# Four block products of a first group's second matmul in seven products instead of eight, with their operand sums made by accumulating DMAs

## The chip, the cores and the metric

The kernel runs on one core of one Trainium2 chip. The metric is the device time of one launch in microseconds; the figure given for a kernel is the median of its runs.

## What is computed

Two stages, in fp32. Attention with routing: queries and keys are assigned to the nearest of 16 centroids, and a query attends only to keys of its own cluster. Then an MLP on the attention's output, and it is this part that the change touches:

```python
x = attn_out.transpose(0, 2, 1, 3).reshape(3072, 512)
h = x @ w_in                                   # w_in: 512 x 2048
g = np.where(h > 0, h, np.exp(np.minimum(h, 0)) - 1)
return g @ w_out                               # w_out: 2048 x 512
```

## The kernel before

After the attention, the 3072 tokens are worked off in six groups of 512, `k_` = 0 to 5. Each group has a first product (`x @ w_in`, with the ELU behind it) and a second product (`g @ w_out`, with a store of the result).

Both products use Strassen's scheme in Winograd's form: a product of two 2x2 block matrices in seven block products instead of eight. `w_out` is kept as seven "quads", which are the right operands of the outer level: `a11`, `a12`, `s1`, `a22` lie in place in the tile `w_out`, and `s2`, `s4`, `s3` lie in parts of the tiles `p_out`, `sums_w` and `words_w`. So a group's second product is seven *units* `UNITS` (n = 0 to 6: M1 with `a11`, M2 with `a12`, M3 with `s4`, M7 with `s3`, M6 with `s2`, M5 with `s1`, M4 with `a22`). A unit is again a 2x2 block product, of 512-deep blocks with 128 columns, and it can be done in two ways:

- *plainly*, in eight small products: for each of four quadrants `q_`, two small products accumulate in a PSUM bank. A small product (`small_product`, line 1042) is four matmuls of 128x128 by 128x128.
- *in sevenths*, by the same scheme once more (`OutUnit`, `chain`): the small products m1 to m7, with sums of the four parts q11, q12, q21, q22 of the left operand (`t_step`, t1 to t4, VectorE) and of the right operand: s1 = q21 + q22, s2 = s1 - q11, s3 = q11 - q21, s4 = q12 - s2. m1, m2 and m4 take q11, q12 and q22 themselves; m5, m6, m7 and m3 take s1, s2, s3 and s4. `chain` interleaves the units: m6, m2, the next unit's m1, m7, the next unit's m5, m3, m4.

In the kernel before, the second product of group 0 is plain throughout (`second_product_plain`), and those of groups 1 to 5 run in sevenths. The right-hand sums of the quads ("`w_out`'s table") are made once, by VectorE, during the first product of group 1 (`table_steps`: seven quads of four operations, two steps at each call of `fill`), and stored to HBM by SyncE's DMA queue (`keep_far`). From then on they are streamed back into ten slots. `s1` overwrites q21 in its quad. A second table, of `w_in`, serves the first products of groups 2 to 5. It is made during the second product of group 0 (`in_table_steps`, 16 VectorE operations, 13 stores and 4 loads on SyncE's queue), with the tile `spare` and the dead columns of `xT` for its results.

The order of the work is written by hand (a manual schedule): each engine runs its own instructions in program order and waits only for what they depend on. A DMA waits on the queue of the engine that issues it, so what stands behind it on that engine waits too. SyncE (SP) issues plain loads and stores, GpSimd (POOL) some others.

Around the change stand: `early_on`, which ends the preparation of `w_out`'s quads in unit 0; `verdict`, a 1x1 matmul in unit 2; `take`, which empties the quadrants' banks into `s_all` (ScalarE for M1, M3, M7) or adds to the output (VectorE); `g_step`, which updates the outer left operands in place; and `next_group(0)` after unit 5, which makes the left sums of group 1's first product in the tile `x_sum` (`x_sum_step`, four POOL operations) and loads its first right-hand sums into `w_tmp` (`w_step`, three SP loads; `w_tmp` is the first half of `spare`, `stage` the second). The first product of group 1 (`unit`) is four units of seven block products (line 796).

Of the kernel before, what the change touches and what calls it, by code (L numbers as in the profile page):

```python
# [14 lines left out]
Act = mybir.ActivationFunctionType  # L15
Alu = mybir.AluOpType
# [3 lines left out]
P = 128  # L20
# [41 lines left out]
def main_path(ctx, tc, c, q, k, v, centroids, moe_w_in, moe_w_out, out):  # L62


    nc = tc.nc
# [7 lines left out]
    KC = DM // P  # L73
    FC = DF // P
    N = B * S
    GS = 512
# [17 lines left out]
    xT = space.tile([P, KC, N], F32, name="xT")  # L94
# [811 lines left out]
    def part_w(a, i, j):  # L906
        return quad_w[a][:, 4 * j : 4 * j + 4, ts(i, P)]

    def part_g(b, i, j):
        return quad_g[b][:, 4 * i : 4 * i + 4, ts(j, P)]  # L910
# [12 lines left out]
    def flat_far(a, x):  # L923
        return far_w[a, x].rearrange("p (f m) -> p f m", m=P)

    def table_steps():


        made = []

        def keep_far():
            for to, src in made:
                nc.sync.dma_start(to, src)
            made.clear()

        for n, a in enumerate(("s3", "s4", "s2", "a11", "a12", "s1", "a22")):
            at = p_out[:, :1536] if n % 2 else s_all
            s3, s2, s4 = (at[:, ts(m, 512)].rearrange("p (f m) -> p f m", m=P) for m in range(3))
            q11, q12, q21, q22 = (part_w(a, i, j) for i in range(2) for j in range(2))
            nc.vector.tensor_tensor(s3, q11, q21, op=Alu.subtract)  # L940
            yield
            nc.vector.tensor_tensor(q21, q21, q22, op=Alu.add)
            keep_far()
            yield
            nc.vector.tensor_tensor(s2, q21, q11, op=Alu.subtract)
            yield
            nc.vector.tensor_tensor(s4, q12, s2, op=Alu.subtract)
            parts = [("s3", s3), ("s2", s2), ("s4", s4)]
            if a not in DIRECT:
                parts += [("q11", q11), ("q12", q12), ("q22", q22), ("s1", q21)]  # L950
            made += [(flat_far(a, x), y) for x, y in parts]
            yield
        keep_far()

    WHICH = {"m1": "q11", "m2": "q12", "m3": "s4", "m4": "q22", "m5": "s1", "m6": "s2", "m7": "s3"}
    HERE = {"m1": (0, 0), "m2": (0, 1), "m4": (1, 1), "m5": (1, 0)}
# [3 lines left out]
    FIRST_IN = 2  # L960
# [12 lines left out]

    def in_table_steps():

        dead = [xT[:, ch, :GS] for ch in range(KC)]
        flat = spare.rearrange("p a n -> p (a n)")
        held = [flat[:, ts(n, 512)] for n in range(6)]
        made = []

        def keep_far():
            for to, src in made:
                nc.sync.dma_start(to, src)
            made.clear()

        for a, s1, (s3, s2, s4) in (
            ("a11", dead[0], held[3:]),
            ("s1", dead[0], dead[1:]),
            ("a12", held[0], held[3:]),
            ("s2", dead[2], held[:3]),  # L990
        ):
            if a == "s2":
                keep_far()
                for n in range(4):
                    nc.sync.dma_start(dead[n], s2_far[:, n // 2, n % 2])
                q11, q12, q21, q22 = dead
            else:
                q11, q12, q21, q22 = (part_in(a, i, j) for i in range(2) for j in range(2))
            nc.vector.tensor_tensor(s3, q11, q21, op=Alu.subtract)
            yield  # L1000
            nc.vector.tensor_tensor(s1, q21, q22, op=Alu.add)
            keep_far()
            yield
            nc.vector.tensor_tensor(s2, s1, q11, op=Alu.subtract)
            yield
            nc.vector.tensor_tensor(s4, q12, s2, op=Alu.subtract)
            made += [(far_in[a, x], y) for x, y in (("s3", s3), ("s2", s2), ("s4", s4))]
            if a == "s2":
                made.append((far_in[a, "s1"], s1))
            yield  # L1010
        keep_far()
# [16 lines left out]
    def weights(of, a, m):  # L1028

        nonlocal used  # L1030
        table = far_w if of == "out" else far_in
        if (a, WHICH[m]) not in table:
            i, j = HERE[m]
            return (part_w if of == "out" else part_in)(a, i, j), lambda: None
        assert streamed[used] is table[a, WHICH[m]]
        slot_ = slots_w[used % len(slots_w)]
        used += 1
        return slot_.rearrange("p (f m) -> p f m", m=P) if of == "out" else slot_, fetch
# [12 lines left out]
    def banks_of(k_, n):  # L1051
        return sets[(k_ + n) % 2]
# [5 lines left out]
    class OutUnit:  # L1058
        of, width = "out", P

        def __init__(self, k_, n):
            self.k_, self.n, self.a = k_, n, UNITS[n][1]
            self.banks = [x[:, :P] for x in banks_of(k_, n)]
            self.m5 = stage[:, 2, ts(n % 2, P)]
            self.u3 = stage[:, 2, 256 + P * (n % 2) : 384 + P * (n % 2)]

        def product(self, m):
            left = t_of[SUM[m]] if m in SUM else part_g(UNITS[self.n][2], *SIDE[m])
            right, done = weights("out", self.a, m)
            small_product(self.banks[BANK[m]], left, right, m in ("m1", "m5"))  # L1070
            done()

        def t(self, t):
            t_step(self.n, t)

        def take(self, q_):
            take(self.k_, self.n, q_)

        def taken(self):
            taken(self.k_, self.n)  # L1080

        def note(self, at):
            k_, n = self.k_, self.n
            if at == "m2" and 1 <= n <= 3:
                g_step(n - 1, 0)
            elif at == "m7" and 1 <= n <= 3:
                g_step(n - 1, 1)
            elif at == "m4" and n == 1:
                next_group(k_)
            elif k_ + 1 == FIRST_IN and at in ("m2", "m7") and n in (4, 5):  # L1090
                x_sum_step(k_ + 1, 2 * (n - 4) + (at == "m7"))
            if at == "m4" and k_ == FIRST_IN - 1 and n < 3:
                in_place(n)
# [209 lines left out]

            behind.append(rest)

    def t_step(n, t):
        b = UNITS[n][2]
        q11, q12, q21, q22 = (part_g(b, i, j) for i in range(2) for j in range(2))
        to = t_of[t]
        if t == "t1":  # L1310
            nc.vector.tensor_tensor(to, q12, q11, op=Alu.subtract)
        elif t == "t2":
            nc.vector.tensor_tensor(to, q22, t_of["t1"], op=Alu.subtract)
        elif t == "t3":
            nc.vector.tensor_tensor(to, q22, q12, op=Alu.subtract)
        else:
            nc.vector.tensor_tensor(to, q21, t_of["t2"], op=Alu.subtract)
# [50 lines left out]
    def store(k_, tiles):  # L1368
        for i in range(2):
            store_tile(k_, 2 * tiles + i, nc.sync)  # L1370

    def next_group(k_):
        if k_ + 1 < N // GS:
            if k_ + 1 != FIRST_IN:
                for n in range(4):
                    x_sum_step(k_ + 1, n)
            for n in range(3):
                if n or k_ + 1 < FIRST_IN:
                    w_step(k_ + 1, 0, n)

    def second_product_plain(k_, early_on):

        in_table = in_table_steps()
        for n in range(len(UNITS)):
            _, a, b = UNITS[n]
            for q_ in range(4):
                for j in range(2):
                    small_product(
                        banks_of(k_, n)[q_],
                        part_g(b, j, q_ % 2),  # L1390
                        part_w(a, q_ // 2, j),
                        j == 0,
                        j == 1,
                    )
                if n == 0 and q_ == 0:
                    flush_all()
                    early_on()
                elif n == 2 and q_ == 1:
                    verdict()
                take(k_, n, q_)  # L1400
                if q_ < 3 and n > 0:
                    next(in_table, None)
            taken(k_, n)
            if n < 3:
                g_step(n, 0)
                g_step(n, 1)
            if n == 5:
                run(in_table)
                next_group(k_)

    def findings():
        ok = c["ok"]
# [55 lines left out]
    def run(steps_of):  # L1468
        for _ in steps_of:
            pass  # L1470
# [12 lines left out]
    for u in range(4):  # L1483
# [5 lines left out]
        elif u == 2:  # L1489
            scale_x(last_n - 1, r_of)  # L1490
            scale_x(last_n, e_of)
    second_product_plain(0, early_on)

    table = table_steps()

    def fill_table():
        next(table, None)
# [2 lines left out]
    for k_ in range(1, N // GS):  # L1500
        if k_ < FIRST_IN:
            for u in range(4):
                if u < 2:
                    blanks((k_ + u) % 2)
                run(unit(k_, u, fill=fill_table))
        else:
            rest_of_group(k_)
        chain(units_behind(k_))
# [261 lines left out]
```

## Time and profile before

| | us |
|---|---|
| median of 3 runs (lowest, highest) | 892.48 (892.21, 892.85) |
| profiled execution: its own time | 893.83 |
| profiled execution: its span, first to last instruction | 892.10 |

| share of the span | PE | VectorE | ScalarE | POOL |
|---|---|---|---|---|
| busy | 99% | 79% | 49% | 25% |

The second product of group 0 runs from 381.45 to 432.34 us of the span, and group 1's first product from there to 482.59 us. The profile is of one execution. A busy PE is read from the starts of its instructions, since their ends are modelled. A wait is charged to the engine or the DMA whose signal came last.

### The profile page before, as it was taken

Reading aid. Unit: us, or ns where it says so; the run is one execution under the profiler, and the core shown is the slowest. Engines: PE = TensorE matmul, PEld = TensorE weight load, DVE = VectorE, ACT = ScalarE, POOL = GpSimd, SP = SyncE. Lnnn points to the kernel's source line nnn. Section 1 sums busy time; section 2 is a strip of 40 time slices with the busy share of each in tenths; the row PEclk is TensorE's granted clock in tenths of the full one; section 3 lists DMA queues with packets and bytes.
Section 4 is the critical chain, followed back from the end, with each engine's and each line's share of the span. In section 5 each row is a group of like instructions: output and inputs, shape, how many; then the busy total and the mean of one; then the engine's idle time right before and its main releaser. Section 6 shows DMA issues by size and latency. Waiting matters only on the chain.

```text
span 892.1 us, 17029 instructions
## 1 busy us (share of the span) xinstructions
PE 880.4 (99%) x6473; PEld 681.1 (76%) x6473; DVE 705.5 (79%) x1021; ACT 440.4 (49%) x833; POOL 225.7 (25%) x289
## 2 busy tenths in 40 slices
PE   8999999999999999999999999999999999999997
PEld 5444444444444458899989999999999999999997
DVE  4789998999998987894588956894689568956784
ACT  5677786787768664410133236423642354225421
POOL 1011121121113566860123003510351025202300
PEclk9999999999999999999999999999999999999999
DMA  7766685466337442113597866186618661866172
GB/s 222 182 128 184 148 179 129 128 120 150 78 119 212 125 142 65 48 47 119 197 323 247 269 215 189 47 268 206 193 48 264 213 195 48 260 212 202 49 228 83
DMA packets 155257, 144.63 MB, mean 162 GB/s; under 512 B 89760, under 2 KB 107168, under 8 KB 154144
## 3 DMA queue, kind: packets, MB, share of 16 engines
q1 hardware_dynamic: 151584, 132.45, 50.1%
q0 software_dynamic: 3296, 10.49, 4.6%
q8 instruction: 53, 0.87, 0.4%
q10 hardware_dynamic: 288, 0.52, 0.2%
q14 instruction: 36, 0.29, 0.1%
HBM read 114.59 MB, written 21.50 MB: 153 GB/s over the span
## 4 chain that ended last, share of the span: by engine, by line
PE 91%; POOL 3%; DVE 2%; issue 2%; DMA 1%; SPq 1%; ACT 0%; POOLq 0%; ACTq 0%
PE bank L1042 23%; PE banks L510 15%; PE o_bank L548 14%; PE bank L796 11%; PE bank L1114 9%; PE o_bank L1042 4%; PE banks L523 4%; PE d_bank L1042 2%; PE o_bank L796 2%; PE o_bank L1114 2%; PE d_bank L568 1%; PE d_bank L438 1%; POOL kq_g L810 1%; PE d_bank L1114 1%; DMA spare<-w_far 1%
## 5 line engine op out<-in xcount | busy, mean ns | idle before, releaser
L532 ACT ACTIVATE p_out<-banks 128x768 f32<-128x768 f32 x192 | 154.0, 811 | 25.4 <-PE banks L523 23.7
L548 PE MATMUL o_bank<-p_out,kq_g 128*64 128x384 f32 x768 | 130.9, 490 | 0.0
L548 PEld LDWEIGHTS o_bank<-p_out,kq_g 128*64 128x64 f32 x768 | 52.3, 137 | 74.8 <-issue 69.7
L810 POOL TENSOR_SCALAR kq_g<-kq_g 128x512 f32<-128x512 f32 x96 | 69.4, 731 | 150.1 <-ACT kq_g L809 149.7
L535 DVE TENSOR_TENSOR sums_w<-p_out 128x1536 f32<-128x1536 f32 x32 | 59.1, 1847 | 10.3 <-ACT p_out L532 10.3
L1042 PE MATMUL bank<-w_out,kq_g 128*128 128x128 f32 x512 | 63.1, 275 | 0.3 <-DVE kq_g L813 0.3
L1042 PEld LDWEIGHTS bank<-w_out,kq_g 128*128 128x128 f32 x512 | 60.5, 192 | 0.8 <-DVE kq_g L813 0.5
L796 PE MATMUL bank<-xT,spare 128*128 128x256 f32 x256 | 59.3, 379 | 0.8 <-DMA spare<-w_far 0.8
L809 ACT ACTIVATE kq_g<-bank 128x512 f32<-128x512 f32 x68 | 39.8, 602 | 38.5 <-PE bank L796 18.4
L540 DVE TENSOR_TENSOR sums_w<-sums_w,p_out 128x1536 f32<-128x1536 f32 x32 | 56.2, 1757 | 3.3 <-DVE sums_w L535 0.5
L609 POOL DMA_DIRECT2D sums_w<-xT x28 | 17.8, 650 | 153.2 <-DVE xT L585 92.0
L796 PEld LDWEIGHTS bank<-xT,spare 128*128 128x128 f32 x256 | 48.2, 190 | 7.5 <-ACT kq_g L809 1.2
L796 PE MATMUL bank<-x_sum,w_in 128*128 128x256 f32 x224 | 52.9, 379 | 0.0
L813 DVE SCALAR_TENSOR_TENSOR kq_g<-kq_g,bank 128x512 f32<-128x512 f32 x68 | 45.0, 680 | 7.7 <-POOL kq_g L810 7.7
L796 PEld LDWEIGHTS bank<-x_sum,w_in 128*128 128x128 f32 x224 | 42.6, 190 | 5.8
L1328 DVE TENSOR_TENSOR kq_g<-kq_g 128x1024 f32<-128x1024 f32 x36 | 45.3, 1264 | 1.5 <-PE bank L1042 1.5
L1132 POOL TENSOR_TENSOR spare<-x_sum 128x128 f32<-128x128 f32 x16 | 7.3, 457 | 154.4 <-PE bank L1114 88.7
L562 ACT ACTIVATE xT<-o_bank 128x384 f32<-128x384 f32 x32 | 15.7, 489 | 53.0 <-PE o_bank L548 53.0
L604 POOL TENSOR_TENSOR xT<-xT,sums_w 128x384 f32<-128x384 f32 x32 | 41.1, 1305 | 1.6 <-DMA sums_w<-xT 1.6
L510 PE MATMUL banks<-x_sum,xT 64*128 64x384 f32 x192 | 39.8, 492 | 0.0
L510 PE MATMUL banks<-kq_g,xT 64*128 64x384 f32 x192 | 39.6, 491 | 0.0
L510 PE MATMUL banks<-x_sum,kq_g 64*128 64x384 f32 x192 | 39.6, 491 | 0.0
(343 smaller groups left out, 1998.8 us busy)
## 6 DMA issues: line engine op xcount, KB each, us to landing
kq_g<-in_v_dram SPq DMA_DIRECT2D x32, 384.0 KB, 3.7
sums_w<-far_s_s SPq DMA_DIRECT2D x42, 256.0 KB, 3.7
spare<-w_far SPq DMA_DIRECT2D x32, 256.0 KB, 3.2
words_w<-far_s_s SPq DMA_DIRECT2D x26, 256.0 KB, 3.1
out_dram<-p_out SPq DMA_DIRECT2D x22, 256.0 KB, 3.4
w_out<-in_q_dram SPq DMA_DIRECT2D x112, 48.0 KB, 2.4
sums_w<-xT POOLq DMA_DIRECT2D x28, 192.0 KB, 3.3
sums_w<-far_s_q SPq DMA_DIRECT2D x21, 256.0 KB, 3.5
```

The source lines that it names most:

```text
L510: nc.tensor.matmul(s[:, e, :HS], lhsT=kT[b % 2][pr][rows, ts(kt, P)], rhs=qT[half][pr][rows], start=True, stop=False,)
L532: nc.scalar.activation(probs[kt], s[:, :, :HS], Act.Exp, scale=SCALE)
L535: nc.vector.tensor_tensor(add_to, probs_all[:, : 4 * HS], probs_all[:, 4 * HS : 8 * HS], op=Alu.add)
L540: nc.vector.tensor_tensor(add_to, add_to, probs_all[:, 8 * HS :], op=Alu.add)
L548: nc.tensor.matmul(o_bank[64 * e : 64 * e + 64, :HS], lhsT=v_raw[n % 2][:, e, kt], rhs=probs[kt][:, e], start=(kt == 0), stop=(kt == NT - 1),)
L604: nc.gpsimd.tensor_tensor(x_of(n), x_of(n), r, op=Alu.mult)
L796: nc.tensor.matmul(bank[:, ts(f, QS)], lhsT=left[:, ch, ts(f, P)], rhs=right[:, ch], start=first and f == 0 and ch == 0, stop=ch == 1, ski ...
L810: nc.gpsimd.tensor_scalar(to, to, 1.0, 0.0, op0=Alu.min, op1=Alu.max)
L813: nc.vector.scalar_tensor_tensor(to, to, -1.0, as_part(bank, to), op0=Alu.add, op1=Alu.max)
L1042: nc.tensor.matmul(bank[:, :P], lhsT=left[:, f], rhs=right[:, f], start=first and f == 0, stop=last and f == 3, skip_group_check=True,)
L1114: nc.tensor.matmul(bank[:, ts(f, P)], lhsT=left[:, ts(f, P)], rhs=right, start=m in ("m1", "m5") and f == 0, stop=True, skip_group_check=True,
L1328: nc.vector.tensor_tensor(b[to][:, f], b[x][:, f], b[y][:, f], op=op)
```

## The change

Units 0 to 2 of group 0's second product stay plain (`second_product_first`). Units 3 to 6 run in sevenths, through `chain`. Their left sums t1 to t4 lie in dead columns of `xT` (`t_first`). Their right sums are made before they are needed:

- for `s3` (unit 3) by four VectorE operations in units 1 and 2 (`table_block`);
- for `s2` and `s1` (units 4, 5), and in part for `a22` (unit 6), by `tables_apart` after unit 0: seven negated copies on ScalarE and twelve accumulating DMAs on POOL's queue, each of 128x512 fp32 (256 KB);
- the rest of `a22` by `table_last`, at unit 4's m4: two negated copies and two accumulating DMAs.

The sums of these four quads go to HBM from here: 20 stores on SP's queue. The table of `w_in` moves into group 1's first product, behind the remaining three blocks of `w_out`'s table (`table_rest`), with its four loads and 13 stores; its results now lie in `p_out` and `s_all` instead of `spare`. `next_group(0)` stands at unit 5's m4.

```diff
+    made = []
+    def keep_far():
...
+    def table_block(a, at):
+        s3, s2, s4 = (x.rearrange("p (f m) -> p f m", m=P) for x in at)
+        q11, q12, q21, q22 = (part_w(a, i, j) for i in range(2) for j in range(2))
+        nc.vector.tensor_tensor(s3, q11, q21, op=Alu.subtract)
+        yield
+        nc.vector.tensor_tensor(q21, q21, q22, op=Alu.add)
+        keep_far()
+        yield
+        nc.vector.tensor_tensor(s2, q21, q11, op=Alu.subtract)
+        yield
+        nc.vector.tensor_tensor(s4, q12, s2, op=Alu.subtract)
...
+    late = [stage[:, 0], sums_w[:, 3584:], stage[:, 1]]
+    apart = {
+        "s2": [in_rows(x) for x in thirds(x_sum)],
+        "s1": [w_tmp[:, m].rearrange("p c n -> p (c n)") for m in range(3)],
+        "a22": [sums_w[:, 3584:], p_out[:, 4096:], stage[:, 0]],
+    }
...
+    def minus_of(to, x):
+        nc.scalar.activation(to, x, Act.Copy, scale=-1.0)
+    def add_far(to, x):
+        nc.gpsimd.dma_start(to, x, accum_op=Alu.add)
+    def tables_apart():
+        for a in ("s2", "s1"):
             q11, q12, q21, q22 = (part_w(a, i, j) for i in range(2) for j in range(2))
+            s3, s2, s4 = apart[a]
+            minus_of(s3, q21)
+            minus_of(s2, q11)
+            minus_of(s4, q22)
+            here[a].update(s2=s2, s3=s3, s4=s4)
+        q11, q12, q21, q22 = (part_w("a22", i, j) for i in range(2) for j in range(2))
+        minus_of(apart["a22"][1], q11)
+        for a in ("s2", "s1"):
...
+            add_far(q21, q22)
+            add_far(s3, q11)
+            add_far(s4, q12)
+        add_far(part_w("a22", 1, 0), part_w("a22", 1, 1))
+        for a in ("s2", "s1"):
+            s3, s2, s4 = apart[a]
+            add_far(s2, part_w(a, 1, 0))
+            add_far(s4, s3)
+        add_far(apart["a22"][1], part_w("a22", 1, 0))
+    def table_last():
+        s3, s2, s4 = apart["a22"]
+        minus_of(s3, s2)
+        minus_of(s4, s2)
+        add_far(s3, part_w("a22", 1, 1))
+        add_far(s4, part_w("a22", 0, 1))
...
+    def table_rest():
+        for n in range(4):
+            nc.sync.dma_start(dead[n], s2_far[:, n // 2, n % 2])
+        for a, at in (
+            ("s4", thirds(s_all)),
+            ("a11", thirds(p_out)),
+            ("a12", thirds(s_all)),
+        ):
+            yield from table_block(a, at)
+        yield from in_table_steps()
...
         def note(self, at):
+            if k_ == 0:
+                if at == "m4":
+                    if n == 3:
+                        g_step(2, 1)
+                        keep_far()
+                    elif n == 4:
+                        table_last()
+                        keep_apart("s2")
+                        keep_apart("s1")
+                    elif n == 5:
+                        keep_apart("a22")
+                        next_group(0)
+                return
...
+    FIRST_OUT = 3
+    first_table = table_block("s3", late)
+    def second_product_first(early_on):
+        for n in range(FIRST_OUT):
...
+                take(0, n, q_)
+                if n == 1 and q_ < 3 or n == 2 and q_ == 0:
+                    next(first_table, None)
+                if n == 2:
+                    t_step(FIRST_OUT, f"t{q_ + 1}", t_first)
+            taken(0, n)
+            if n == 0:
+                tables_apart()
+            for part in range(2 - n // 2):
+                g_step(n, part)
+        chain([(OutUnit, 0, n) for n in range(FIRST_OUT, len(UNITS))])
...
-    second_product_plain(0, early_on)
-
-    table = table_steps()
+    second_product_first(early_on)
+    table = table_rest()
```

More of the change, by code (lines that the diff above doesn't have):

```diff
@@ L924, in flat_far @@
         return far_w[a, x].rearrange("p (f m) -> p f m", m=P)
[L926 to L938, printed above, removed]
-            q11, q12, q21, q22 = (part_w(a, i, j) for i in range(2) for j in range(2))
[L940 to L952, printed above, removed]
-        keep_far()
+    made = []
@@ new lines, in keep_far @@
+    def keep_far():
+        for to, src in made:
+            nc.sync.dma_start(to, src)
+        made.clear()
+    def table_block(a, at):
[9 more added lines that the diff above has]
+        nc.vector.tensor_tensor(s4, q12, s2, op=Alu.subtract)
+        parts = [("s3", s3), ("s2", s2), ("s4", s4)]
+        here[a].update(parts)
+        if a not in DIRECT:
+            parts += [("q11", q11), ("q12", q12), ("q22", q22), ("s1", q21)]
+        made.extend((flat_far(a, x), y) for x, y in parts)
+        yield
@@ new lines, in main_path, with thirds, in_rows @@
+    here = {a: {} for a in quad_w}
+    dead = [xT[:, ch, :GS] for ch in range(KC)]
+    t_first = {
+        f"t{n + 1}": x.rearrange("p (f n) -> p f n", n=P) for n, x in enumerate(dead)
+    }
+    def thirds(x):
+        return [x[:, ts(m, 512)] for m in range(3)]
+    def in_rows(x):
+        return x.rearrange("p (f m) -> p f m", m=P)
+    late = [stage[:, 0], sums_w[:, 3584:], stage[:, 1]]
[3 more added lines that the diff above has]
+        "a22": [sums_w[:, 3584:], p_out[:, 4096:], stage[:, 0]],
+    }
@@ new lines, in main_path @@
+    apart = {a: [x if len(x.shape) == 3 else in_rows(x) for x in at] for a, at in apart.items()}
+    def minus_of(to, x):
[4 more added lines that the diff above has]
+        for a in ("s2", "s1"):
+            q11, q12, q21, q22 = (part_w(a, i, j) for i in range(2) for j in range(2))
+            s3, s2, s4 = apart[a]
[6 more added lines that the diff above has]
+        for a in ("s2", "s1"):
+            q11, q12, q21, q22 = (part_w(a, i, j) for i in range(2) for j in range(2))
+            s3, s2, s4 = apart[a]
[4 more added lines that the diff above has]
+        for a in ("s2", "s1"):
+            s3, s2, s4 = apart[a]
+            add_far(s2, part_w(a, 1, 0))
+            add_far(s4, s3)
+        add_far(apart["a22"][1], part_w("a22", 1, 0))
@@ new lines, in table_last, with keep_apart @@
+    def table_last():
[4 more added lines that the diff above has]
+        add_far(s4, part_w("a22", 0, 1))
+        here["a22"].update(s2=s2, s3=s3, s4=s4)
+    def keep_apart(a):
+        s3, s2, s4 = apart[a]
+        parts = [("s3", s3), ("s2", s2), ("s4", s4)]
+        if a not in DIRECT:
+            for x, at in (("q11", (0, 0)), ("q12", (0, 1)), ("q22", (1, 1)), ("s1", (1, 0))):
+                parts.append((x, part_w(a, *at)))
+        made.extend((flat_far(a, x), y) for x, y in parts)
+        keep_far()
@@ L974, in in_table_steps @@
     def in_table_steps():
[L976 to L990, printed above, removed]
+        for a, s1, at in (
+            ("s2", dead[2], p_out),
+            ("a11", dead[0], s_all),
+            ("s1", dead[0], p_out),
+            ("a12", dead[0], s_all),
         ):
+            s3, s2, s4 = thirds(at)
             if a == "s2":
-                keep_far()
-                for n in range(4):
-                    nc.sync.dma_start(dead[n], s2_far[:, n // 2, n % 2])
                 q11, q12, q21, q22 = dead
@@ L1006, in in_table_steps @@
             nc.vector.tensor_tensor(s4, q12, s2, op=Alu.subtract)
-            made += [(far_in[a, x], y) for x, y in (("s3", s3), ("s2", s2), ("s4", s4))]
+            made.extend((far_in[a, x], y) for x, y in (("s3", s3), ("s2", s2), ("s4", s4)))
             if a == "s2":
@@ L1063, in __init__ @@
             self.banks = [x[:, :P] for x in banks_of(k_, n)]
+            self.t_of = t_of if k_ else t_first
             self.m5 = stage[:, 2, ts(n % 2, P)]
@@ L1067, in product @@
         def product(self, m):
-            left = t_of[SUM[m]] if m in SUM else part_g(UNITS[self.n][2], *SIDE[m])
-            right, done = weights("out", self.a, m)
+            left = self.t_of[SUM[m]] if m in SUM else part_g(UNITS[self.n][2], *SIDE[m])
+            if self.k_ == 0:
+                at, done = here[self.a], lambda: None
+                right = at[WHICH[m]] if WHICH[m] in at else part_w(self.a, *HERE[m])
+            else:
+                right, done = weights("out", self.a, m)
             small_product(self.banks[BANK[m]], left, right, m in ("m1", "m5"))
@@ L1073, in t @@
         def t(self, t):
-            t_step(self.n, t)
+            t_step(self.n, t, self.t_of)
         def take(self, q_):
@@ L1304, in rest_of_group, with t_step @@
             behind.append(rest)
-    def t_step(n, t):
+    def t_step(n, t, t_of=t_of):
         b = UNITS[n][2]
@@ L1370, in store, with x_sums, w_sums @@
             store_tile(k_, 2 * tiles + i, nc.sync)
+    def x_sums(k_):
+        for n in range(4):
+            x_sum_step(k_, n)
+    def w_sums(k_):
+        for n in range(3):
+            if n or k_ < FIRST_IN:
+                w_step(k_, 0, n)
     def next_group(k_):
@@ L1374, in next_group @@
             if k_ + 1 != FIRST_IN:
[L1375 to L1384, printed above, removed]
+                x_sums(k_ + 1)
+            w_sums(k_ + 1)
+    FIRST_OUT = 3
+    first_table = table_block("s3", late)
+    def second_product_first(early_on):
+        for n in range(FIRST_OUT):
             _, a, b = UNITS[n]
@@ L1388, in second_product_plain @@
                     small_product(
-                        banks_of(k_, n)[q_],
+                        banks_of(0, n)[q_],
                         part_g(b, j, q_ % 2),
@@ L1399, in second_product_plain @@
                     verdict()
[L1400 to L1409, printed above, removed]
+                take(0, n, q_)
[9 more added lines that the diff above has]
+        chain([(OutUnit, 0, n) for n in range(FIRST_OUT, len(UNITS))])
     def findings():
@@ L1505, in main_path @@
                 run(unit(k_, u, fill=fill_table))
+            run(table)
         else:
```

## The prediction

> **What bounds the kernel now.** I read the page's busy times, the windows by stage, TensorE's timeline, its waits, and the chain.
>
> ```profile
> PE 880.4 (99%) x6473; PEld 681.1 (76%) x6473; DVE 705.5 (79%) x1021; ACT 440.4 (49%) x833; POOL 225.7 (25%) x289
> ```
> Windows (stretch, length, then busy us of PE, PEld, DVE, ACT, POOL; clock; DMA share; GB/s):
> ```profile
> 396.29:403.75 7.46, 7.46 (x68) 7.31 (x67) 5.42 (x9) 0.80 (x3) 0.00 (x0) 1.00 0.31 115
> 403.75:432.34 28.59, 28.59 (x259) 28.58 (x258) 12.77 (x29) 1.33 (x5) 0.00 (x0) 1.00 0.44 147
> 432.34:482.59 50.25, 49.45 (x231) 42.95 (x229) 39.11 (x56) 17.52 (x31) 11.49 (x15) 1.00 0.88 292
> ```
> The second row is units 3 to 6, which the change remakes: TensorE never pauses, VectorE works less than half of it, ScalarE and POOL hardly. So time there is bought only with TensorE work. TensorE's timeline of two quadrants of unit 5, then of two small products of group 1's chain (start, duration):
> ```profile
> 418.04 1.95 PE L1042 MATMUL bank<-w_out,kq_g 128*128 128x128 f32 x16
> 419.83 1.95 PE L1042 MATMUL o_bank<-w_out,kq_g 128*128 128x128 f32 x16
> ...
> 483.48 1.06 PE L1042 MATMUL d_bank<-w_out,p_out 128*128 128x128 f32 x8
> 484.37 1.06 PE L1042 MATMUL o_bank<-words_w,p_out 128*128 128x128 f32 x8
> ```
> Starts count, as matmuls overlap: a quadrant (two small products, 16 records) takes 1.79 us, a small product 0.893 us, in either way. TensorE's waits in 370 to 490 us are three:
> ```profile
> PE bank L796 <- DMA spare<-w_far: 0.8, 1, 0.8
> PE o_bank L796 <- DVE o_bank L852: 0.3, 1, 0.3
> PE bank L1042 <- DVE kq_g L813: 0.3, 1, 0.3
> ```
> The chain shows what the first of them hangs on: stores of the table on SP's queue, ahead of a load.
> ```profile
> 457.68 1.07 SPq L933
> 458.80 1.10 SPq L933
> 460.01 5.10 DMA spare<-w_far
> 465.24 1.97 PE bank L796 x8
> ```
>
> **TensorE's work.** Units 3 to 6 are 4 x 8 = 32 small products before, 4 x 7 = 28 after. Removed: 4 x 0.893 = 3.57 us. The chain's order costs nothing where it runs already: six stretches of seven products in group 1 (484.37 to 521.89 us) are 6.25 us each with TensorE busy throughout. So, if nothing is late, from 403.75: m1 and m5 of unit 3 until 405.54, unit 3's turn until 411.79, unit 4's until 418.04, unit 5's until 424.29, unit 6's five products until 428.76 (432.34 before).
>
> **Left sums and VectorE.** Gone from the stage: 16 table operations (0.68 us each, L999 to L1006). Added: four for `s3` (0.7 to 1.0, as L940 to L947), sixteen t sums (0.75, L1311 to L1317), eight bank adds (0.29, L1209 and L1221). t1 of unit 3 is free to run when unit 1's `g_step` ends (399.1 before), so the four end near 403, and t1 is needed at 404.65. In unit 3's turn VectorE has about 5.6 us for 6.25; group 1's turns hold up to 6.16 of 6.25 without a pause of TensorE. Cost: 0, covered by TensorE's own work.
>
> **Copies on ScalarE.** Seven of 128x512, 0.6 us each and 0.49 from start to start (L809), behind M1's last copy at 389.34: until about 393. ScalarE's next work was at 398.27, so the cover is its own idle time. Cost 0.
>
> **The accumulating DMAs.** Twelve behind each other on POOL. No row shows one of this shape: q21, q22, q11, q12 are 512-byte rows. The nearest is L1441, two adds of 512 KB into `w_in` with 4 KB rows:
> ```profile
> L1441 POOL DMA_DIRECT2D w_in<-w_in x2: 1079/1212/1345, 270.3 to 271.0; - x2
> DMA to landing us min/median/max: 5.5/6.8/8.2
> ```
> And the DMA view of 273 to 276 us (packets, MB, share of 16 engines), the adds alone:
> ```profile
> q0 software_dynamic: 167, 0.62, 106.8%
> ```
> That is 206 GB/s, so 262 KB take 1.27 us. In 512-byte rows, the table's stores ran at 288 GB/s (444.5 to 446.5), against 407 for 2 KB rows (434 to 435.5): a factor of 1.41, so 1.8 us. I take 1.6 us, ends 1.27 and 1.8. Issue: 1.2 us each; L780 rises from 0.575 to 0.752 us when the pieces double from 128 to 256, so for 512 pieces up to 1.75; I take 1.4. The Trainium skill, "DMA: Bandwidth & Descriptors", section "SWDGE vs HWDGE vs iDMA", says that accumulating is for GpSimd's path only; that it was issued there is what this trace shows too. Its "Rules for kernel authors" ask that an add which meets an earlier one's bytes waits for that one's semaphore: so adds 8 to 12 wait for landings of 1 to 7. These are long past when their turn comes, if an add takes 1.6 us.
>
> First transfer at about 391.7 (first copy 390.2, issue 1.2 to 1.4). The eighth add (`s2`'s s2) lands at 391.7 + 8 x 1.6 + 1.5 = 406.0; the 1.5 us is what L780's landing of 2.3 has over its transfer. It is needed by m6 of unit 4 at 411.8. The twelfth (`a22`'s s2) lands at 412.4. Behind it ScalarE's two copies of `table_last` stand, from 416.3, behind unit 5's m5 copy; behind these, ScalarE's copy of b2 to b3, for which m7 waits at 420.7. So the twelfth may land until 419.2: up to **2.17 us per add** the cover holds, and both my ends lie under it. The last two adds: copies done at 417.6, landings at about 422 and 424.5; m7 and m3 of unit 6 want them at 426.1 and 427.0. Cost 0; the ends are 0 and, from the rival below, several us.
>
> **SP's queue and POOL behind it.** Added: 20 stores, moved away 13 stores and 4 loads. The skill's "Queues, rings and completion order" says that an engine of the DMA takes turns between queues by packets. The trace does not bear that out for adds: in 275 to 277.4 us only q0 moved anything, and a load of `v` issued then landed after 9.5 us, where 3.7 is usual. So the stores are held up while adds run. Work in DMA time: adds about 19, stores of `s3` 5.6 (3 x 0.68 + 4 x 0.9), `s2` 5.6, `s1` 2.0, the last adds 3.2, `a22`'s stores 2.0: 37.4 us from 391.7, so 429 us. The first load of `w_tmp` stands behind these, lands at about 431, and is wanted by group 1's third block product at 428.76 + 0.43 (blanks) + 2 x 1.73 = 432.65. Cost 0 at my value; at 1.8 us per add about +1.3 us.
>
> POOL's four `x_sum_step`s ran at 387 to 394.4; now they come behind the last add, at about 420.5 to 427.5. t1 is wanted at 430.9. "SBUF — State Buffer", section "Who interferes with whom", says that VectorE with two SBUF inputs blocks with a reading GpSimd instruction; the trace agrees (two `g_step` halves took 3.90 us beside them, 2.35 alone). VectorE has slack in units 5 and 6; `g_step` of unit 0 gets quicker. Cost 0.
>
> **Group 1's first product.** VectorE's 28 table steps stay 28. On SP, unit 1 now has 3 + 3 stores where 7 + 7 stood ahead of the `w_far` loads. These loads should be issued about 4 us earlier, and the wait of 0.80 us go. What is late next is TensorE itself. Gain 0.80; lower end 0. The four loads of `dead` come before the first store: 1 MB, 2.7 us, with seven us of room.
>
> **Sum.** 3.57 + 0.80 = 4.37 us. Against the profiled execution's own 893.83 (span 892.10 and 1.73 around it): 889.46. The median shown is 1.35 under that execution: **888.1 us**.
>
> **Rivals.**
> - *An add costs more than 2.17 us* (512-byte rows read twice and written may cost more than the factor of plain stores, or their issue does). Then ScalarE waits in `table_last`, TensorE at unit 5's m7, by 12 us for each us over it. It eats the 4.37 from 2.53 us on, and is slower by over 0.2% from 2.7. At 2.8: 12 x 0.63 = 7.6, 895.7 us. For it: no add of this shape was seen. Against: twice the byte price would be needed. 0.18.
> - *Between*: adds of 2.3 to 2.65 us, within 0.2%: about 892. 0.12.
> - *SP's backlog*: `w_tmp` lands up to 1.5 us late: 889.6. For it: the stage's DMA has little air left in my sum. 0.17.
> - *The wait at 465 stays* in some form, as the DMAs there are still 80% busy: 888.9. 0.13.
> - My forecast, 888.1: 0.40.
> - The change could fail to remove products; the code leaves no room for that.
>
> **Numbers.** What a measurement can tell here is about 0.2%, 1.8 us. Faster 0.70 (forecast, wait that stays, backlog), same 0.12, slower 0.18. The range goes from 887.5 to 893.4: above it lie most cases of the first rival, below it only a pause of TensorE that I have not seen could lie. The first three cases alone: 887.7 to 890.0.
>
> **What would show it.** Right: line-1042 starts at 0.893 us without gaps from 403.75, blanks at about 428.8, no wait on `w_far` in group 1, adds landing within 4 us of their issue or of the one before. Wrong: TensorE waiting in units 4 to 6 for a DMA into `x_sum`, `w_tmp` or `sums_w`, or for ScalarE behind the copies; the third block product of group 1 waiting for `w_tmp`; or the stage as long as before.

## The result and the profile after: slower, 896.50 us

The changed kernel takes **896.50 us** (median of 8 runs, 896.13 to 900.33) against 893.17 for the kernel before on the same chip (8 runs): a ratio of 1.0047, 95% interval 1.0030 to 1.0064. The ratio counts every run, and two of the eight took 900.24 and 900.33 at a mean granted clock of 0.994 and 0.993 (0.995 to 0.998 in the others), for which no trace was kept; the medians alone give 1.0037. The forecast was 888.1, its range ended at 893.4. The profiled execution has its own time of 896.54 and a span of 894.8.

The products are gone as planned: the records of TensorE fall from 6473 to 6437 in the page's line of busy times (four small products are 32 records; some records can be missing from a trace). Its busy time stays at 880.3 us all the same, and its share falls, since the span grew.

```profile
PE 880.3 (98%) x6437; PEld 680.6 (76%) x6441; DVE 709.0 (79%) x1033; ACT 448.8 (50%) x858; POOL 241.0 (27%) x303
```

The windows of the profile after, cut at the pauses that follow (columns as before: stretch, length, busy us of PE, PEld, DVE, ACT, POOL; clock; DMA share; GB/s):

```profile
404.03:412.06 8.03, 8.03 (x74) 8.01 (x72) 3.01 (x6) 2.35 (x9) 2.18 (x2) 1.00 1.24 196
412.06:420.29 8.23, 5.44 (x34) 5.30 (x33) 3.61 (x6) 0.85 (x4) 1.28 (x1) 0.79 1.18 211
420.29:426.71 6.42, 5.53 (x51) 5.34 (x49) 4.20 (x10) 1.90 (x6) 0.45 (x1) 1.00 1.06 274
426.71:436.21 9.50, 8.60 (x72) 8.28 (x73) 7.63 (x18) 1.15 (x5) 7.92 (x6) 1.00 0.99 226
436.21:485.70 49.49, 49.39 (x231) 43.30 (x231) 39.12 (x56) 17.53 (x31) 11.55 (x15) 1.00 0.87 295
```

The first row is unit 3's turn: TensorE full, as forecast. The second row holds 34 records where 8.23 us have room for some 74, and a granted clock of 0.79; the third has one pause, the fourth two. The last row is group 1's first product, which no longer waits: 436.21 to 485.43 us is 49.2, where 50.25 stood. TensorE's waits after, between 370 and 490 us:

```profile
PE bank L1108 <- DMA x_sum<-p_out: 2.8, 1, 2.8
PE bank L1108 <- ACT bank L1286: 0.9, 1, 0.9
PE bank L1108 <- DVE p_out L1419: 0.5, 1, 0.5
PE bank L1108 <- DMA spare<-w_out: 0.4, 1, 0.4
```

The line for `w_far` is gone, and four new ones stand in units 4 to 6. The first is the eighth accumulating DMA, for which unit 4's m6 waits. The second is ScalarE, which stands in `table_last` behind the twelfth, as its own timeline shows:

```profile
425.34 0.63 ACT L975 ACTIVATE sums_w<-p_out 128x512 f32<-128x512 f32 x1 [3.69 <-DMA p_out<-w_out]
```

The third is VectorE, late beside POOL's `x_sum_step`s (unit 6's t3 took 2.78 us there), and the fourth the last accumulating DMA. TensorE's timeline shows what the first pause brought with it (start, duration, eight records of one small product):

```profile
415.02 1.13 PE L1108 MATMUL bank<-x_sum,xT 128*128 128x128 f32 x8 [2.79 <-DMA x_sum<-p_out]
415.99 1.57 PE L1108 MATMUL bank<-p_out,kq_g 128*128 128x128 f32 x8
417.35 1.91 PE L1108 MATMUL bank<-w_out,kq_g 128*128 128x128 f32 x8
419.06 1.40 PE L1108 MATMUL bank<-x_sum,xT 128*128 128x128 f32 x8
420.29 1.06 PE L1108 MATMUL d_bank<-w_out,xT 128*128 128x128 f32 x8
```

The starts are up to 1.71 us apart instead of 0.893: from 416.35 to 419.76, for 3.41 us, the granted clock was 0.5 (called the half clock from here on). From 415.02 to 420.29 are 5.27 us for four products that take 3.57: 1.70 us lost to the clock.

**The balance.** The stage from unit 3's chain to the blanks (matmuls of zeros ahead of group 1's first product) takes 32.2 us (404.03 to 436.21), where 28.6 stood and 25.0 was forecast. By starts, the four pauses are 2.96 + 1.05 + 0.69 + 0.61 = 5.31, the clock 1.70, together 7.0 of the 7.2 over the forecast. Against the kernel before, the stage is 3.6 us longer (32.2 for 28.6), group 1's first product is 1.0 shorter, and the chain starts 0.3 later: about 2.8 us more, and the spans differ by 2.7.

What the adds did is in the row of their line in the profile after, from issue to landing:

```profile
DMA to landing us min/median/max: 4.6/11.9/18.8
```

and in the DMA view of 407 to 412 us (queue, packets, MB, share of 16 engines):

```profile
q0 software_dynamic: 886, 0.48, 78.4%
q1 hardware_dynamic: 883, 0.44, 44.2%
```

q0 carries the adds, q1 SyncE's stores of 512-byte rows. One packet of one, one packet of the other. It was not so all the time. From 396.5 to 399.5 us q0 ran alone:

```profile
q0 software_dynamic: 794, 0.39, 126.6%
```

That is 2.0 us for the 256 KB of an add. The view lists no packet of q1, though a store of SyncE had been issued at 395.97; it landed after 7.2 us, where the one issued at 392.35 took 3.8.

The eighth add lands at 415.0 (forecast 406.0), the twelfth at 425.3 (412.4). By the prediction's own sum (a start at 391.7, 1.5 us for the landing) both make 2.7 us per add, against 1.6 in the working and a cover of 2.17.

### The profile page after: what moved, and what is told of

Read it like the earlier page. It is cut to its first block, busy times and chain, and to the rows that moved or that the text cites. A ratio compares the mean times of both kernels' runs of the same rounds, so it can differ in the third digit from the quotient of the medians.

```text
span 894.8 us, 17058 instructions
## 1 busy us (share of the span) xinstructions
PE 880.3 (98%) x6437; PEld 680.6 (76%) x6441; DVE 709.0 (79%) x1033; ACT 448.8 (50%) x858; POOL 241.0 (27%) x303
## 4 chain that ended last, share of the span: by engine, by line
PE 88%; issue 3%; POOL 3%; DMA 3%; DVE 1%; ACT 0%; SPq 0%; POOLq 0%; ACTq 0%
PE bank L1108 20%; PE banks L510 14%; PE o_bank L548 14%; PE bank L796 12%; PE bank L1198 9%; PE o_bank L1108 4%; PE banks L523 4%; PE o_bank L796 2%; DMA w_out<-w_out 2%; PE d_bank L1108 2%; PE o_bank L1198 2%; PE d_bank L568 1%; PE d_bank L438 1%; POOL kq_g L810 1%; DMA spare<-w_out 1%
## 5 line engine op out<-in xcount | busy, mean ns | idle before, releaser
L1108 PE MATMUL bank<-w_out,kq_g 128*128 128x128 f32 x448 | 56.9, 278 | 0.3 <-DVE kq_g L813 0.3
L1108 PEld LDWEIGHTS bank<-w_out,kq_g 128*128 128x128 f32 x448 | 54.2, 194 | 0.8 <-DVE kq_g L813 0.5
```

The lines of the kernel that those rows point to most:

```text
L1108: nc.tensor.matmul(bank[:, :P], lhsT=left[:, f], rhs=right[:, f], start=first and f == 0, stop=last and f == 3, skip_group_check=True,)
```

## The experiments

Two things could have held units 4 to 6: the adds (their own price, or the stores between them), and POOL's `x_sum_step`s beside VectorE, which the prediction costed at nothing. Ratios are to the kernel before, on the same chip, with 95% intervals. "Pauses" are TensorE's new waits in units 3 to 6.

| run | edit of the changed kernel | us | ratio | pauses, us |
|---|---|---|---|---|
| after | none | 896.50 | 1.0047 (1.0030 to 1.0064) | 2.8, 0.9, 0.5, 0.4 |
| e1 | eight row stores later | 895.61 | 1.0035 (1.0023 to 1.0047) | 1.0, 0.8, 0.2 |
| e2 | copies for adds | 895.31 | 1.0029 (1.0019 to 1.0039) | 4.2 |
| e4 | first pause filled | 897.06 | 1.0043 (1.0031 to 1.0055) | 2.6 |
| e6 | no adds | 890.18 | 0.9971 (0.9959 to 0.9984) | 1.5 |
| e7 | no adds, `x_sum` on VectorE | 889.11 | 0.9956 (0.9941 to 0.9971) | none |
| e8 | `x_sum` on VectorE | 896.38 | 1.0042 (1.0026 to 1.0057) | 2.8, 1.0, 0.4, 0.2 |
| e9 | `s2` and `x_sum` on VectorE | **888.62** | 0.9954 (0.9941 to 0.9968) | none |
| e10 | `s2` on VectorE | 896.09 | 1.0035 (1.0022 to 1.0048) | 5.3 |
| e11 | row stores later, `x_sum` on VectorE | 892.42 | 0.9995 (0.9987 to 1.0004) | 1.0, 0.7 |
| e12 | adds in 2 KB rows, `x_sum` on VectorE | 906.58 | 1.0149 (1.0132 to 1.0166) | 14.3 in unit 1 |

**The stores out of the adds' way (e1).** The eight stores with 512-byte rows (q11, q12, q22 and s1 of `s3` and `s2`) go behind `next_group(0)`'s loads.

```diff
+        if a == "s3":
+            put_off.extend((flat_far(a, x), y) for x, y in parts[3:])
+            parts = parts[:3]
...
-                parts.append((x, part_w(a, *at)))
+                put_off.append((flat_far(a, x), part_w(a, *at)))
...
                         next_group(0)
+                        made.extend(put_off)
+                        keep_far()
```

> The eight stores with 512-byte rows (q11, q12, q22 and s1 of s3 and of s2) are issued behind next_group(0)'s loads instead of at units 3 and 4; all else as in the changed kernel. Theory A (the adds are late because SP's stores take turns with them in the DMA engines): alone, the adds move 265 pieces of 512 bytes in a microsecond, 1.93 us each, so the eighth lands near 410 and the twelfth near 417; TensorE's pauses in units 4 to 6 shrink from 5.3 us to under 1, the clock stays up, and the time is 889 to 890.5 us (6 to 7 below the changed kernel, 0.3 to 0.5% under before). Theory B (an add in 512-byte rows is too slow by itself): the twelfth still lands after 420 and at least 3 us of pause stay, 893.5 to 896 us.

The stage falls by 4.5 us (404.26 to 432.0), the clock stays up, and the twelfth add lands about 3.3 us earlier (422.0). But the time falls by under one: the eight stores are now issued at 431 to 438 us, ahead of group 1's later loads. TensorE's waits in e1:

```profile
PE bank L796 <- DMA spare<-w_far: 1.8, 1, 1.8
PE bank L796 <- DMA spare<-s_far: 1.3, 1, 1.3
```

So the stores are one part of the adds' lateness, and some remains without them: two pauses of about 1 us. The time falls into theory B's range only through the two waits in group 1, which neither theory had.

**The adds' price and the pauses themselves (e2, e4, e6).** e2 issues plain copies in place of the adds, e6 issues nothing.

```diff
-        nc.gpsimd.dma_start(to, x, accum_op=Alu.add)
+        nc.gpsimd.dma_start(to, x)        # e2
+        return                            # e6
```

> Left out: the addition. POOL's fourteen DMAs copy instead of accumulating, with the same shapes, order and waits, so the tables hold other values. Both theories: a piece then costs about 30 ns instead of 72, the twelfth lands before 412, and the time is 888.5 to 890 us. If instead POOL's issue (1.3 us for 512 pieces) or its waits in order for earlier landings set the time (theory C), the pauses stay above 2 us and the time above 892.

> Left out: all fourteen accumulating DMAs, so the right-hand sums of s2, s1 and a22 are only the negated copies. What is left is the forecast's other terms: 28 small products for 32 (3.57 us) and the wait on w_far in group 1 gone (0.8 to 1.0). If these hold, the stage from 404 to the blanks is 25.0 to 25.3 us and the time 888.4 to 889.2. If the chain in group 0 has a cost of its own (ScalarE's copies, VectorE, the left sums), the stage is over 26 us.

In e2 the waits for adds vanish, as they must, and the time hardly moves, 5 us above what both theories expected: one new wait of 4.2 us stands in their place, `PE bank <- DVE xT`, for unit 6's t1. POOL has come to its four `x_sum_step`s at 418.9, and VectorE's operations beside them take up to four times as long. Pause and time are those of theory C, but its cause, POOL's DMA issue, is not: the wait is VectorE's. That was the first sight of the second cause. e6 has the same wait, 1.5 us, and so missed its forecast by 1 us (a stage of 26.8 us, 890.18); its steps begin earlier (415.7) and fall less on unit 6's t sums.

e4 fills the first pause with 17 blank matmuls, into a bank of unit 4 and ahead of its m6, to take the half clock away. The result then holds other values than the changed kernel's, and only the time is used.

```diff
+            if u.of == "out" and u.k_ == 0 and u.n == 4:
+                for _ in range(17):
+                    nc.tensor.matmul(
+                        banks_of(0, 4)[0][:, P:],
+                        lhsT=blank,
+                        rhs=blank[:, 0:1].to_broadcast([P, 384]),
+                        start=True,
+                        stop=True,
+                    )
```

> Seventeen bf16 matmuls of zeros, 128x384, into unused columns of a bank stand ahead of unit 4's m6, about as long as the wait there (2.8 us). If the half clock of 416.4 to 419.8 us follows from that pause, it goes, four small products run at 0.893 us again, and the time falls by 1.7 us to 894.8. If it has another cause, the time stays at 896.5 or rises by what the filler overshoots.

The first pause was filled and the half clock behind it gone, but TensorE only came sooner to the next bar, the twelfth add's landing at about 425.3: a pause of 2.6 us there, and a half clock behind that one. The median did not fall. So the half clock follows from the pauses and isn't a cause of its own. What it costs apart from them isn't shown: two of e4's six executions had a mean granted clock of 1.000 and took 895.25 and 895.84 us, the others 897.00 to 898.21.

**Both causes, one by one and together (e7 to e10).** The `x_sum_step`s go to VectorE, at unit 6's m7 (e7, e8, e9); the four sums of `s2` are made by VectorE behind unit 2's left sums instead of five adds, which leaves seven adds in the first lot (e9, e10).

```diff
-        by = nc.gpsimd if k_ not in (0, FIRST_IN) else nc.vector
+        by = nc.gpsimd if k_ not in (0, 1, FIRST_IN) else nc.vector    # e7, e8, e9
...
-        for a in ("s2", "s1"):
+        for a in ("s1",):                                             # e9, e10
...
-                        next_group(0)
+                        w_sums(1)                                     # e7, e8, e9
+                elif at == "m7" and n == 6:
+                    x_sums(1)
...
+    second_table = table_block("s2", thirds(x_sum))                   # e9, e10
...
+            if n == 2:
+                run(second_table)
```

> Left out: all fourteen accumulating DMAs, as in the run without adds; besides, group 1's four x_sum_steps go from POOL to VectorE, in unit 6 at m7. Theory D (POOL's x_sum_steps, which now fall beside units 5 and 6, hold up VectorE, and with it t1 of unit 6): TensorE's 1.5 us wait for L1395 goes, the stage is 25.0 to 25.3 us, and the time 888.4 to 889.2. If VectorE is late by its own work in units 5 and 6, the wait stays over 1 us and the time at 890 or above.

> The changed kernel with group 1's four x_sum_steps on VectorE, in unit 6 at m7; nothing else. The adds end the waits, so the twelfth still lands near 425 and the stage keeps its length: 895.5 to 896.5 us, at most 1 us under the changed kernel. If POOL's steps beside VectorE were the main loss, it is 892 or less.

> s2's four sums by VectorE behind unit 2's left sums (2.7 us, in its idle time), so that seven adds are left in the first wave instead of twelve; x_sum_steps on VectorE. If an add costs 1.93 us alone and up to 2.7 with stores beside it, the seventh lands at 392 + 7 x 1.93..2.7 + 2 = 407.5 to 413, before table_last wants it at 416.3: no pause over 0.5 us, the clock stays up, 888.5 to 890 us, 0.3 to 0.5% under before. If SP's stores or a wait in group 1 take it back, 890 to 893.

> As the kernel with s2's sums on VectorE, but x_sum_steps stay on POOL. By theory D this keeps a wait of 1.5 to 4 us on VectorE's t sums or bank adds in units 5 and 6: 890.5 to 893 us. If theory D is wrong, it equals its partner, 888.5 to 890.

Each cause is enough by itself. e8 takes only POOL's work away and keeps the adds: 896.38, pauses nearly as in the changed kernel. e10 makes the adds early and keeps POOL's work: 896.09, with one pause of 5.3 us, longer than the 1.5 to 4 expected, and the half clock behind it. Take both away, and e9 has no pause: its chain runs from 403.89 in steps of 0.893 to the blanks at 429.12, and it takes 888.62 us. e7, without any adds, confirms it at 889.11. The window of the stage in e9:

```profile
403.89:429.12 25.23, 25.18 (x227) 25.10 (x227) 18.29 (x41) 6.33 (x23) 3.48 (x3) 1.00 1.04 256
```

e9 and e10 differ only in the four `x_sum_step`s: POOL does them from 418.58 in e10, VectorE from 427.88 in e9. Of VectorE's timeline, unit 5's t4, the two sums of `taken` behind M6 and unit 6's t1, first in e10:

```profile
417.75 3.73 DVE L1399 TENSOR_TENSOR xT<-kq_g,xT 128x512 f32<-128x512 f32 x1 [0.60 <-PE bank L1107]
421.91 2.91 DVE L1436 TENSOR_TENSOR sums_w<-sums_w 128x512 f32<-128x512 f32 x2
424.74 1.74 DVE L1393 TENSOR_TENSOR xT<-kq_g 128x512 f32<-128x512 f32 x1
```

and in e9:

```profile
418.38 0.69 DVE L1401 TENSOR_TENSOR xT<-kq_g,xT 128x512 f32<-128x512 f32 x1 [0.60 <-PE bank L1107]
419.51 1.29 DVE L1438 TENSOR_TENSOR sums_w<-sums_w 128x512 f32<-128x512 f32 x2
420.72 0.69 DVE L1395 TENSOR_TENSOR xT<-kq_g 128x512 f32<-128x512 f32 x1
```

POOL's steps in e10:

```profile
418.58 2.34 POOL L746 TENSOR_TENSOR x_sum<-xT 128x512 f32<-128x512 f32 x1
421.00 1.60 POOL L748 TENSOR_TENSOR x_sum<-xT,x_sum 128x512 f32<-128x512 f32 x1
422.56 1.71 POOL L750 TENSOR_TENSOR xT<-xT 128x512 f32<-128x512 f32 x1
424.23 1.70 POOL L752 TENSOR_TENSOR x_sum<-xT,x_sum 128x512 f32<-128x512 f32 x1
```

The same four instructions of VectorE take 8.4 us in e10 and 2.7 in e9. POOL's steps end at 420.92, 422.60, 424.27 and 425.93; the three slow lines end at 421.48, 424.82 and 426.48, each 0.55 us behind one of these ends. So here an operation of 0.69 us comes through when one of POOL's is over. That is no rule for every overlap: in e6 a t sum that started 0.1 us before POOL's first step took its 0.69 us.

**What of the adds is price, what is sharing (e11, e12).** e11 is e8 with e1's eight stores put behind units 0 and 1 of group 1; e12 is e8 with adds of whole 2 KB rows.

```diff
+                if u < 2:                                             # e11
+                    for to, src in put_off[4 - 4 * u : 8 - 4 * u]:
+                        nc.sync.dma_start(to, src)
...
-            q11, q12, q21, q22 = (part_w(a, i, j) for i in range(2) for j in range(2))
+            q11, q12, q21, q22 = (rows(a, n) for n in range(4))       # e12
```

> The four x_sum steps run on VectorE (at unit 6's m7) and the eight stores of 512-byte rows of SyncE's queue (q11, q12, q22 and q21 + q22 of s2 and of s3) are issued in group 1's first product, behind its units 0 and 1. All twelve accumulating DMAs stay as they are. Theory A (the stores that take turns with the adds are what makes the twelfth add late): the twelfth lands by about 419, no wait of TensorE over 1 us in units 4 to 6, 889 to 890.5 us. Theory B (the adds' own price, about 1.93 us each without company, is enough): the twelfth lands at 420 to 422, pauses of 1 to 2 us at unit 4's m6 and unit 5's m7 stay, 892 to 895 us. If VectorE beside POOL were the only other cause, e8's 896.4 would fall by less than 1 us.

> As the changed kernel with the four x_sum steps on VectorE, but the accumulating DMAs take whole rows of 2 KB (contiguous 128x512 pieces of the quads' tiles) where they took four rows of 512 bytes in each partition. So other numbers are added up: the right-hand sums of s2, s1 and a22 hold other values, with the same count of instructions and bytes. If the price of the pieces decides: 128 pieces of 187 ns are 1.5 us per add instead of 1.93, the twelfth add lands near 412 to 416, no wait of TensorE over 1 us, 888.6 to 890.5 us. If the stores' turns decide whatever the row: the twelfth lands behind 420 and the time stays at 893 to 896.5 us.

e11 came out at the edge of the second theory: 892.42 us, the twelfth add at 421.6. TensorE's waits in e11:

```profile
PE bank L1111 <- DMA x_sum<-p_out: 1.0, 1, 1.0
PE bank L796 <- DMA spare<-w_far: 1.0, 1, 1.0
PE bank L1111 <- ACT bank L1291: 0.7, 1, 0.7
```

So with POOL's steps out of the way, taking the eight stores from between the adds brings 4.0 us (e8's 896.38 to 892.42, of which 1.7 is the half clock), and the change comes out even and no more. To e9's 888.62 are another 3.8, of which 3.2 can be placed: the adds' own price with the stores that stay keeps the stage 2.2 us longer than e9's (27.2 against 25.0, to the last product's end), and TensorE waits 1.0 for a `w_far` load in group 1, where the stores put off now stand. The adds' rate is read where nearly nothing else runs; from the DMA view of e11, 402 to 405 us:

```profile
q0 software_dynamic: 770, 0.38, 118.8%
```

and of e12, 396 to 400 us:

```profile
q0 software_dynamic: 388, 0.73, 111.0%
```

0.38 MB in 3 us make 2.0 to 2.1 us per add of 512 pieces, as in the stretch of the profile after where q0 ran alone; in 2 KB rows 0.73 MB in 4 us make 1.44 us per add. Single packets took 72 ns (median) for 512 bytes and 187 ns for 2 KB. e12's time says nothing of the schedule: whole rows of the tile `w_out` hold `a22` and `a12` side by side, so its adds write where unit 1 reads, and TensorE waits for them for 14.3 us (`PE bank <- DMA w_out<-w_out`). It missed its expected time for that reason, and only the price is taken from it; whether the whole change with 2 KB rows would hold the forecast stays open.

## Why the prediction was wrong

- **Right: the products.** 3.57 us. In e9 the stage is 25.0 us from the first start to the last product's end, as worked out, and its time is 4.2 under the kernel before (892.82 in its batch), where 4.37 was forecast.
- **Right: group 1's wait, 0.80.** It is gone after, and the first product is 1.0 shorter.
- **Right: chain, copies and left sums by themselves.** e7 has all of them and no pause. ScalarE's copies cost nothing until they stood behind a late add.
- **Wrong: an add costs 1.6 us, at most 1.8.** Its own price is 2.0 (after, e11), near 1.44 only in 2 KB rows (e12). Two of the twelve, s4 with s3 added, do have 2 KB rows (256 packets of that size in the profile after), which the working did not set apart. The factor of 1.41, from plain stores of 512 and 2048 bytes, sat on the 1.27 us of adds with 4 KB rows: that made 1.8, which as the dearer end was still too low. The piece was priced as if it were a store, while a piece of 512 bytes costs 72 ns as an add and 28 to 32 as a store. At 2.0 the cover of 2.17 would just have held, so this alone did not fail the prediction.
- **Wrong: "the stores are held up while adds run".** This is the step that broke the cover. The Trainium skill ("DMA: Bandwidth & Descriptors", section "Queues, rings and completion order") had turns by packets, and the prediction set that aside for one stretch of the profile before in which only q0 moved and a load of `v` lay behind adds. That load also stood behind a load of 1 MB in its own queue (issued at 273.93, landed after 9.0 us), so its 9.5 us were not the adds' doing alone. The profile after shows both: q0 alone from 396.5 to 399.5 us, and 886 packets beside 883 from 407 to 412. What decides between the two isn't shown; the adds' packet size (4096 bytes and 335 ns before, 512 bytes after) does not by itself, as the short ones ran alone too. Over the whole stretch the stores took their turns, and an add took 2.7 us. The prediction's own figures tell what hung on it: the 11.2 us of `s3`'s and `s2`'s stores, put among the adds, would move the twelfth landing from 412.4 to 423.6 at most (an estimate), past the 419.2 that the cover allowed. The prediction's first rival was priced at 2.8 us per add and 895.7 us, and given 0.18. Its reason, an add dear by itself, was not what came, and the place where it would be felt was only half right, as the eighth add stopped TensorE before the twelfth stopped ScalarE.
- **Wrong: POOL's `x_sum_step`s cost 0.** The skill's "SBUF — State Buffer", section "Who interferes with whom", was cited, and the trace before agreed (3.90 against 2.35 us); the cover was "slack in units 5 and 6" without a sum. e10 prices it: 8.4 us instead of 2.7 for t4, the two sums of `taken` and t1, in VectorE's order, and TensorE waits 5.3 us for the last. In the changed kernel the late adds hid most of this (only the third pause, 0.5 us, is VectorE's), so e8 hardly shows it.
- **Missing: the clock.** No term stood for it. It took 1.70 us in the profile after; in e10 the clock was at half for 6.8 us, part of them in the pause. The rival at 2.8 us per add came near the result without it, so that agreement is partly chance.

What is not separated: how much of the 2.2 us by which e11's stage exceeds e9's is the adds' price, how much the stores of 2 KB rows that stay between them, and how much POOL, which waits for landings before it issues adds 10 to 12 (8.5 us in all in the profile after). A part is the stores': in e11 the eleventh add landed at 417.7, and while the twelfth was still under way, from 418 to 422 us, SyncE's queue moved 538 packets (0.97 MB) and POOL's 117.

## What to carry to other kernels

Price an accumulating DMA by its pieces, at the row length that it has, and check what other queue will be busy beside it: here the two queues moved 886 and 883 packets in 5 us, so the cover had to hold at the shared rate, 2.7 us per add, and not at the 2.0 of an add alone. When work moves to POOL's idle time, list VectorE's operations with two SBUF inputs in that stretch and price them as held up by POOL's durations (8.4 us for 2.7 in e10) if they are on a chain. And where two causes hide each other, removing one shows nothing: undo both before either is called harmless.

## What was not expected of the hardware

- An accumulating DMA is carried in packets of its own row length (512 bytes: 72 ns, 512 packets per 256 KB; 2 KB: 187 ns; 4 KB: 335 ns), while plain copies of the same tiles on the same queue (e2) went as 4096-byte packets of 224 ns.
- Waits of TensorE of 2.6 to 2.8 us (2.75 to 2.96 from one product's end to the next start) were enough for a half clock of 3.41 us (after, e4, e8); waits of up to 1.8 us brought none (e1, e6, e11). The skill, "TensorE: Matmul & The Clock Gate", section "What's actually happening", gives a free-running window of 3413 ns and a drop after at least one idle window of about 3.4 us. The length of the half clock, 3.41 us, agrees; the drop here came after shorter pauses.
